# Half of the down projection's results added into SBUF by accumulating DMAs

## The chip, the cores and the metric

The kernel runs on one core of a Trainium2 chip. The time is device time in microseconds (us) of one execution. Before the change the median of 3 runs is 921.73 us (920.55 to 922.61).

## The reference

Attention with capped scores, then a mixing of tokens, then a feed-forward block with a residual, in float32 on 4 batches, 12 heads, 448 tokens and head width 64 (model width 768, hidden width 3072):

```
scores = cap * tanh(scale * q @ k.T / cap)          # per batch and head, 448 x 448
attn   = exp(scores - max) / (sum + 1e-9)
x      = (attn @ v) as [batch, 448, 768]
u      = x + (x.T @ U @ V).T                        # U: 448 x 32, V: 32 x 448
out    = u + relu(u @ w_ch1) @ w_ch2                # w_ch1: 768 x 3072, w_ch2: 3072 x 768
```

## The kernel before

The result of each batch b is built in one SBUF tile `u_bufs[b]`, 128 partitions x 6 slices d x 448 tokens, float32; slice d holds 128 of the 768 features. Attention and mixing fill it, and the feed-forward block adds to it in place, chunk by chunk.

The hidden width is cut into 24 blocks f of 128, and these into 12 chunks c of two (`CF`). For each chunk the up products make g = relu(...), 128 x 448, kept as a high and a low part, and the down products multiply the two blocks of w_ch2 with them. A down product of one d is 6 matmuls into one PSUM bank (`products`, L823: two f, and for each high x high, high x low, low x high). Its result is then added by VectorE to slice d (`add`, L828). This is done in two passes. In the plain pass (n = 0, batches 0 and 1) `moe` makes, for each chunk and batch, the up products of both f (`up_plain`, L738, 18 matmuls each), and between them all six down products of the chunk and batch before. In the Strassen pass (n = 1, batches 2 and 3) `up_seven` makes the up products of both batches and both f by seven products (L759, 9 matmuls each) with combinations on VectorE (L771, L776), and after each of them two of the twelve down products of the chunk before are taken. After the last chunk of a pass (`last`) each slice is stored (L834).

PSUM has eight banks. In the plain pass three of them (`pm`) serve the up and down products; in the Strassen pass five more (`pl`) join them. g is made by ScalarE (relu, high part) and VectorE (low part, L723). In the plain pass each weight block is decoded from 64-bit words by VectorE and ScalarE (L270 to L283), split into high (L229 on ScalarE) and low (L654), and written to DRAM (`kept`), from where the Strassen pass reads it again (L617).

Attention of batches 0 and 1 comes first; that of batches 2 and 3 is woven into the plain pass, a pair of heads every 50 us in the plan. The normalisation of a pair is a chain on GpSimd's DMA queue: four transfers of the sums into r (L480), VectorE's reciprocal (L490), one transfer to DRAM, rd (L485), and four broadcast loads, rb (L498). VectorE multiplies u by rb (L502), and then TensorE transposes u for the mixing (L525).

The order of instructions on every engine is drawn up beforehand. Each piece of work is a task with the engines it can run on and an assumed duration in ns, the buffers that it reads and writes, and a priority (smaller first). `simulate` plays the tasks through, engine by engine, and a task starts only when its buffers are free; the kernel then issues everything in that order. Each engine works through its own queue in order, so an instruction that waits holds up those behind it. The add has priority -200, ahead of all else:

```
self.task({"DVE": 622}, add, r=[(ps, 0)], w=[(u, d)], prio=-200)
```

Of the kernel before, what the change touches and what calls it, by code (L numbers as in the profile page):

```python
# [11 lines left out]
F32 = mybir.dt.float32  # L12
# [4 lines left out]
ALU = mybir.AluOpType  # L17

B, H, S, D = 4, 12, 448, 64
# [20 lines left out]
class Pool:  # L40


    def __init__(self, name, bufs, after=(), space=None, side=None):
        self.name, self.bufs, self.after, self.space, self.side = name, bufs, after, space, side
        self.free = dict(bufs)
        self.due = 0
        self.stack = self.pool = None
# [188 lines left out]
class Build(Plan):  # L236
    def __init__(self, tc, qk, v, u, vv, w1, w2, cap, ident, out):
        super().__init__()
        self.tc, self.nc = tc, tc.nc
        self.qk, self.v, self.u, self.vv = qk, v, u, vv  # L240
        self.w, self.cap, self.id_dram, self.out = (w1, w2), cap, ident, out
        PSUM = bass.MemoryType.PSUM
        self.cp = Pool("cp", {"const": 1})
        self.up = Pool("up", {"u%d" % b: 1 for b in range(B)})
        self.wp = Pool("wp", {"wa": 2, "w1": 3, "g": 3})
        self.wq = Pool("wq", {"wr": 2, "w0": 2})
        self.pre = Pool("pre", {"th": 4, "qk": 1, "es": 2})
        self.hp = Pool("hp", {"hl": 2}, after=(self.pre,))
        self.ap = Pool("ap", {"qk": 3, "vn": 2, "th": 3, "es": 2, "sr": 1, "r7": 2, "rb": 2, "xh": 1, "xl": 1, "ys": 1},
            side="right")  # L250
        self.xp = Pool("xp", {"x": 4, "ws": 3, "g": 3, "wa": 1}, after=(self.hp, self.wq))
        self.late = Pool("late", {"x": 3, "ws": 4, "cx": 4, "ta": 3}, after=(self.ap,), side="right")
        self.px = Pool("px", {"sc": 1, "s": 1}, space=PSUM, side="right")
        self.ps = Pool("ps", {"sc": 1, "o": 1, "misc": 2}, space=PSUM)
        self.pm = Pool("pm", {"mm": 3}, after=(self.px,), space=PSUM, side="right")
        self.pl = Pool("pl", {"mm": 5}, after=(self.ps,), space=PSUM)
        self.dp = None
# [421 lines left out]
    def moe(self):  # L679
# [4 lines left out]
        for n, bs in enumerate(((0, 1), (2, 3))):  # L684
            xs = self.operands(bs) if n else {b: self.halves(b) for b in bs}
            for c in range(NCH):
                fs = [c * CF + i for i in range(CF)]
                begin, prio = (12000, ALONE - 4 - 100) if n == 0 and c == 0 else (0, 3)
                ws = self.strassen_weights(c, prio) if n else {f: self.weights(0, f, True, begin, prio) for f in fs}
                w1 = {f: self.weights(1, f, n == 0, begin, prio) for f in fs}  # L690
                gs = {}
                if n:
                    down = self.down(order, *pend) if pend else iter(())
                    if c == 0:
                        for _ in down:
                            pass
                        order += 12
                    for _ in self.up_seven(bs, fs, xs, ws, gs, order):
                        next(down, None)
                        next(down, None)  # L700
                    for _ in down:
                        pass
                    pend = bs, fs, w1, gs, c == NCH - 1, n
                    order += 20
                    continue
                for b in bs:
                    for i, f in enumerate(fs):
                        self.up_plain(b, f, xs[b], ws[f], gs, order, n)
                        order += 1
                        if i == 0 and pend:  # L710
                            for _ in self.down(order, *pend):
                                pass
                            order += 12
                    pend = (b,), fs, w1, gs, c == NCH - 1, n
# [95 lines left out]
    def down(self, order, bs, fs, w1, g, last, n):  # L810
        nc = self.nc
        for i, b in enumerate(bs):
            u = self.u_bufs[b]
            for d in range(ND):
                k = ND * i + d
                at = order + 1 + k // 2 * 3 + k % 2
                ps = self.bank(n)
                sl = slice(128 * d, 128 * d + 128)

                def products(ps=ps, sl=sl, b=b):  # L820
                    for f in fs:
                        for i, (wi, gi) in enumerate(((0, 0), (0, 1), (1, 0))):
                            nc.tensor.matmul(  # L823
                                ps.t[:, :S], w1[f].t[:, wi, sl], g[b, f].t[:, gi], start=f == fs[0] and i == 0,
                                stop=f == fs[-1] and i == 2)

                def add(ps=ps, d=d, u=u):
                    nc.vector.tensor_tensor(out=u.t[:, d], in0=u.t[:, d], in1=ps.t[:, :S], op=ALU.add)  # L828

                self.task({"PE": 6 * 206}, products, r=[(x, i) for f in fs for x in (w1[f], g[b, f]) for i in range(2)],  # L830
                    w=[(ps, 0)], prio=at, mode="mm")
                self.task({"DVE": 622}, add, r=[(ps, 0)], w=[(u, d)], prio=-200)
                if last:
                    self.task({"SP": 350}, lambda b=b, d=d, u=u: nc.sync.dma_start(  # L834
                        out=self.out[b, 128 * d:128 * d + 128], in_=u.t[:, d]), r=[(u, d)], lat=2500, prio=-200)
                yield
# [56 lines left out]
```

## Time and profile before

| | before |
|---|---|
| median of 3 runs | 921.73 us |
| span of the profiled execution | 921.8 us |
| TensorE (PE) matmuls busy | 898.0 us, 97% |
| VectorE (DVE) busy | 714.1 us, 77% |
| ScalarE (ACT) busy | 379.9 us, 41% |
| GpSimd (POOL) busy | 60.5 us, 7% |
| bytes moved by DMA | 104.58 MB |

The profile is of one execution; its own time is the span of 921.8 us, which is within the spread of the runs. Busy time is the time in which an engine had an instruction in work; matmuls overlap, so a row's mean duration of a matmul is longer than the time from one to the next. A row of the tables by stage has the stretch in us, the busy time of each engine with the number of its instructions in brackets, the granted TensorE clock as a share of full speed (PEclk), the mean share of time in which the 16 DMA engines were busy, and GB/s. A line of the timeline has the start, the duration, the engine, the line of the kernel, the operation, what it writes and reads, and in square brackets the idle time before it and what ended it.

### The profile page before, as it was taken

What the parts mean: (1) busy time and instruction counts of PE and PEld (TensorE: products, weight loads), DVE (VectorE), ACT (ScalarE), POOL (GpSimd) and SP (SyncE); (2) the same over time, 40 slices, a digit from 0 to 9 for tenths busy, and PEclk for the clock granted to TensorE, in tenths of its full rate; (3) what the DMA queues carried; (4) which work ended last, traced back from release to release, by engine and by line L of the source; (5) the groups of instructions that cost most, each with busy time, mean ns of one, the idle gap of its engine ahead of it and who ended that gap; (6) DMA issues with size and microseconds to landing.
All of it is one profiled execution on the core that took longest, in us unless ns stands there. A gap on an engine that the chain in (4) does not pass through costs nothing.

```text
span 921.8 us, 11491 instructions
## 1 busy us (share of the span) xinstructions
PE 898.0 (97%) x4428; PEld 704.5 (76%) x4428; DVE 714.1 (77%) x1119; ACT 379.9 (41%) x513; POOL 60.5 (7%) x112
## 2 busy tenths in 40 slices
PE   6999999999999998999999999899999999999998
PEld 2233375767767666599999998799999999999997
DVE  5798896887887876778898775977777777777755
ACT  6988755545354541724323232512332222332210
POOL 0322210101011111020000000000000000000000
PEclk9999999999999998999999999999999999999999
DMA  7546330545434426145445433221121121122103
GB/s 255 173 153 204 92 101 32 163 175 169 167 125 149 138 61 211 66 137 181 121 156 190 163 103 123 100 72 67 52 69 56 48 61 60 52 69 67 38 1 120
DMA packets 34262, 104.58 MB, mean 113 GB/s; under 512 B 6192, under 2 KB 10272, under 8 KB 34208
## 3 DMA queue, kind: packets, MB, share of 16 engines
q1 hardware_dynamic: 23072, 79.29, 27.6%
q10 hardware_dynamic: 6912, 18.88, 5.1%
q0 software_dynamic: 4224, 5.68, 2.2%
q8 instruction: 35, 0.57, 0.3%
q14 instruction: 19, 0.16, 0.1%
HBM read 79.28 MB, written 24.47 MB: 113 GB/s over the span
## 4 chain that ended last, share of the span: by engine, by line
PE 90%; DMA 4%; DVE 4%; issue 1%; ACT 1%; POOL 0%; SPq 0%; DVEq 0%; POOLq 0%
PE mm L823 37%; PE mm L738 18%; PE mm L759 15%; PE sc L396 7%; PE o L436 4%; PE misc L436 2%; PE o L423 2%; PE misc L540 2%; DMA qk<-in_qk 1%; PE misc L525 1%; DMA r<-sr 1%; DMA rb<-rd 1%; DMA rd<-r 1%; PE misc L561 1%; PE misc L475 1%
## 5 line engine op out<-in xcount | busy, mean ns | idle before, releaser
L823 PE MATMUL mm<-g,w 128*128 128x448 f32 x1728 | 376.3, 368 | 0.5 <-DVE g L723 0.4
L823 PEld LDWEIGHTS mm<-g,w 128*128 128x128 f32 x1728 | 322.3, 188 | 44.5 <-issue 8.2
L828 DVE TENSOR_TENSOR u<-u,mm 128x448 f32<-128x448 f32 x288 | 177.7, 622 | 54.5 <-PE mm L823 50.5
L738 PE MATMUL mm<-hl,w 128*128 128x448 f32 x864 | 189.4, 371 | 0.0
L738 PEld LDWEIGHTS mm<-hl,w 128*128 128x128 f32 x864 | 160.2, 189 | 28.9 <-issue 14.9
L759 PE MATMUL mm<-x,ws 128*128 128x448 f32 x756 | 166.4, 368 | 3.7 <-DVE ws L597 3.6
L759 PEld LDWEIGHTS mm<-x,ws 128*128 128x128 f32 x756 | 142.4, 189 | 16.9 <-DVE ws L597 4.4
L401 ACT ACTIVATE th<-sc 128x896 f32<-128x896 f32 x84 | 75.2, 917 | 57.5 <-PE sc L396 43.4
L396 PE MATMUL sc<-qk 64*128 64x448 f32 (+1 forms) x384 | 87.1, 595 | 7.3 <-DVE qk L376 6.1
L229 ACT ACTIVATE w<-wa 128x768 fp32r<-128x768 f32 x72 | 59.4, 838 | 57.3 <-PE mm L823 35.7
L409 ACT ACTIVATE th<-th,capt 128x1792 f32<-128x1792 f32 (+1 forms) x48 | 76.7, 1603 | 0.7
L771 DVE TENSOR_TENSOR cx<-cx,mm 128x448 f32<-128x448 f32 x60 | 37.2, 620 | 45.8 <-PE mm L759 45.8
L654 DVE TENSOR_TENSOR w<-wa,w 128x768 fp32r<-128x768 f32 x72 | 68.6, 952 | 1.3 <-ACT w L229 0.3
L270 ACT ACTIVATE wa<-wr 128x768 f32<-128x768 f32 (+2 forms) x50 | 44.8, 896 | 55.7 <-DVE w L654 43.1
L274 DVE TENSOR_SCALAR wr<-wr 128x768 uint16<-128x768 uint16 (+2 forms) x50 | 50.6, 1024 | 17.1 <-DMA wr<-in_w 14.9
L396 PEld LDWEIGHTS sc<-qk 64*128 64x128 f32 (+1 forms) x384 | 27.1, 178 | 41.9 <-issue 14.7
L445 DVE TENSOR_TENSOR es<-es,th 128x896 f32<-128x896 f32 (+1 forms) x48 | 52.1, 1084 | 6.8 <-ACT th L409 6.3
L229 ACT ACTIVATE ws<-ta 128x384 fp32r<-128x384 f32 x39 | 20.3, 523 | 75.6 <-PE mm L759 69.3
L279 DVE TENSOR_SCALAR wr<-wr 128x768 uint16<-128x768 uint16 (+2 forms) x50 | 50.7, 1022 | 0.2
L229 ACT ACTIVATE g<-mm 128x448 fp32r<-128x448 f32 x48 | 26.1, 543 | 60.1 <-PE mm L738 60.1
L436 PE MATMUL o<-th,vn 128*64 128x448 f32 x216 | 47.5, 561 | 3.3 <-ACT th L409 3.0
L283 DVE SCALAR_TENSOR_TENSOR wa<-wa,wr 128x768 int32<-128x768 int32 (+2 forms) x50 | 46.5, 931 | 2.6 <-ACT wa L270 2.4
(77 smaller groups left out, 597.3 us busy)
## 6 DMA issues: line engine op xcount, KB each, us to landing
wr<-in_w SPq DMA_DIRECT2D x48, 768.0 KB, 5.5
kept<-wa ACTq DMA_DIRECT2D x48, 384.0 KB, 5.7
wa<-kept SPq DMA_DIRECT2D x48, 384.0 KB, 3.1
qk<-in_qk SPq DMA_DIRECT2D x24, 448.0 KB, 5.8
vn<-in_v SPq DMA_DIRECT2D x12, 448.0 KB, 7.3
rb<-rd POOLq DMA_DIRECT2D x48, 112.0 KB, 3.8
out_t<-u SPq DMA_DIRECT2D x24, 224.0 KB, 1.9
r<-sr POOLq DMA_DIRECT2D x48, 1.8 KB, 2.7
```

What stands on the lines that cost most here:

```text
L229: e.activation(out=out, in_=in_, func=func)
L279: nc.vector.tensor_scalar(out=half[:, 1::4], in0=half[:, 3::4], scalar1=0x8000, scalar2=None, op0=ALU.bitwise_and)
L396: nc.tensor.matmul(ps.t[out, a, :S], qks[c].t[hd, 1, 128 * t:min(S, 128 * t + 128)], qks[c].t[hd, 0], start=True, stop=True)
L401: nc.scalar.activation(out=th.t[:, j], in_=ps.t[:, :, :S], func=AF.Tanh)
L409: nc.scalar.activation(out=th.t[:, :n], in_=th.t[:, :n], func=AF.Exp, scale=self.capt)
L436: nc.tensor.matmul(o.t[64 * a:64 * a + 64, :S], vn.t[:, 3 * i + t, a], th.t[:, j, a], start=t == 0 and not late, stop=t == 2 and late)
L445: e.tensor_tensor(out=out(), in0=in0(), in1=in1(), op=ALU.add)
L654: e.tensor_tensor(out=w.t[:, 1], in0=a.t, in1=w.t[:, 0].bitcast(F32), op=ALU.subtract)
L738: nc.tensor.matmul(ps.t[:, :S], w.t[:, wi, sl], hl.t[:, xi, d], start=d == 0 and i == 0, stop=d == ND - 1 and i == 2)
L759: nc.tensor.matmul(ps.t[:, :S], ws[p].t[:, wi, sl], xs[p].t[:, xi, d], start=n == 0, stop=n == 8)
L823: nc.tensor.matmul(ps.t[:, :S], w1[f].t[:, wi, sl], g[b, f].t[:, gi], start=f == fs[0] and i == 0, stop=f == fs[-1] and i == 2)
L828: nc.vector.tensor_tensor(out=u.t[:, d], in0=u.t[:, d], in1=ps.t[:, :S], op=ALU.add)
```

## The change

Where d is odd and the chunk isn't the last of its pass, the result of the down product is copied by ScalarE from PSUM to a staging tile `st` (two of them, 128 x 448 float32, in the pool `wp`), and a DMA issued by GpSimd adds the staging tile into slice d of u in SBUF. The plan counts 560 ns of ScalarE for the copy, 1100 ns of GpSimd for the issue, and 3000 ns until the sum has landed. All other results are added by VectorE as before.

```diff
-        self.wp = Pool("wp", {"wa": 2, "w1": 3, "g": 3})
+        self.wp = Pool("wp", {"wa": 2, "w1": 3, "g": 3, "st": 2})
...
-                self.task({"DVE": 622}, add, r=[(ps, 0)], w=[(u, d)], prio=-200)
+                if d % 2 and not last:
+                    st = self.buf("st", [128, S], F32, self.wp)
+
+                    def pour(st=st, d=d, u=u):
+                        nc.gpsimd.dma_start(out=u.t[:, d], in_=st.t, accum_op=ALU.add)
+
+                    self.task({"ACT": 560}, lambda st=st, ps=ps: self.copy(nc.scalar, st.t, ps.t[:, :S]), r=[(ps, 0)],
+                        w=[(st, 0)], prio=-200)
+                    self.task({"POOL": 1100}, pour, r=[(st, 0)], w=[(u, d)], lat=3000, prio=-200)
+                else:
+                    self.task({"DVE": 622}, add, r=[(ps, 0)], w=[(u, d)], prio=-200)
```

## Rows read from the trace of the kernel before

**Rows 1.** Page, part 1: busy us, share of the span, instructions.
```profile
PE 898.0 (97%) x4428; PEld 704.5 (76%) x4428; DVE 714.1 (77%) x1119; ACT 379.9 (41%) x513; POOL 60.5 (7%) x112
```
**Rows 2.** Table by stage: woven stage, plain pass alone, Strassen pass.
```profile
130.00:420.00 290.00, 285.57 (x1424) 203.55 (x1423) 222.78 (x310) 132.73 (x163) 30.47 (x54) 0.99 0.42 136
420.00:575.00 155.00, 154.91 (x761) 142.45 (x760) 125.35 (x184) 48.49 (x72) 0.00 (x0) 1.00 0.45 147
603.00:903.00 300.00, 300.00 (x1473) 276.39 (x1472) 225.01 (x404) 78.20 (x136) 0.00 (x0) 1.00 0.18 54
```
**Rows 3.** Table by stage: 5 us stretches around two gaps of TensorE.
```profile
355.00:360.00 5.00, 2.85 (x14) 2.16 (x12) 2.49 (x5) 0.00 (x0) 0.00 (x0) 1.00 0.58 136
360.00:365.00 5.00, 3.88 (x11) 2.05 (x12) 4.92 (x10) 2.25 (x3) 0.00 (x0) 0.58 0.01 3
365.00:370.00 5.00, 5.00 (x22) 3.63 (x21) 1.79 (x3) 1.79 (x2) 0.00 (x0) 0.73 0.74 236
595.00:600.00 5.00, 1.35 (x6) 0.94 (x5) 5.00 (x11) 3.60 (x7) 0.00 (x0) 0.98 0.26 79
600.00:605.00 5.00, 5.00 (x19) 4.52 (x18) 3.65 (x7) 0.95 (x2) 0.00 (x0) 0.68 0.53 167
```
**Rows 4.** Timeline from 335 to 362 us, the lines of one normalisation chain.
```profile
343.64 0.56 POOL L485 DMA_DIRECT2D rd<-r  x1 [4.43 <-DVE r L490]
...
350.28 2.54 POOL L498 DMA_DIRECT2D rb<-rd  x4 [6.08 <-DMA rd<-r]
...
357.51 0.62 DVE L502 TENSOR_TENSOR u<-u,rb 128x448 f32<-128x448 f32 x1 [4.42 <-DMA rb<-rd]
...
358.28 0.29 PE L525 MATMUL misc<-ident,u 128*112 128x128 f32 x1 [0.73 <-DVE u L502]
...
359.96 0.61 DVE L502 TENSOR_TENSOR u<-u,rb 128x448 f32<-128x448 f32 x1
```
**Rows 5.** Table by stage: the stretch in which rb was on its way.
```profile
350.00:355.00 5.00, 5.00 (x26) 4.47 (x26) 3.10 (x5) 0.85 (x1) 2.54 (x4) 1.00 1.01 397
```
**Rows 6.** Timeline from 572 to 606 us, TensorE at the second gap's end.
```profile
599.41 2.69 PE L759 MATMUL mm<-x,ws 128*128 128x448 f32 x7 [3.65 <-DVE ws L597]
```
**Rows 7.** Page, part 5: group, count, busy us, mean ns, idle before it.
```profile
L828 DVE TENSOR_TENSOR u<-u,mm 128x448 f32<-128x448 f32 x288 | 177.7, 622 | 54.5 <-PE mm L823 50.5
```
**Rows 8.** Groups by line, ScalarE, 580 to 900 us.
```profile
L229 ACT ACTIVATE cx<-mm 128x448 f32<-128x448 f32 x24 | 13.1, 545 | 41.4 <-PE mm L759 41.4
```
**Rows 9.** Chain that ended last, one piece (start, us), and timeline, one exp.
```profile
431.17 7.30 PE mm L823 x36
...
213.01 1.79 ACT L409 ACTIVATE th<-th,capt 128x1792 f32<-128x1792 f32 x1
```
**Rows 10.** Groups by line, GpSimd, the whole span.
```profile
L480 POOL DMA_DIRECT2D r<-sr x48 | 26.7, 563 | 246.9 <-ACT sr L229 176.7 <-DVE sr L231 70.1
```
**Rows 11.** Instructions of tile rb: from issue to landing of its loads.
```profile
DMA to landing us min/median/max: 2.6/3.8/7.4
```
**Rows 12.** Page, part 6: DMA issues, count, KB each, median us to landing.
```profile
wa<-kept SPq DMA_DIRECT2D x48, 384.0 KB, 3.1
...
out_t<-u SPq DMA_DIRECT2D x24, 224.0 KB, 1.9
r<-sr POOLq DMA_DIRECT2D x48, 1.8 KB, 2.7
```
**Rows 13.** Timeline from 94 to 98.5 us, GpSimd and VectorE.
```profile
94.45 3.48 POOL L480 DMA_DIRECT2D r<-sr  x4 [6.06 <-ACT sr L229]
94.96 1.90 DVE L274 TENSOR_SCALAR wr<-wr 128x768 uint16<-128x768 uint16 x2
```
**Rows 14.** Timeline from 905 to 910 us, stores and adds of the last chunk.
```profile
905.97 3.34 SPq L834 DMA_DIRECT2D out_t<-u  x4
907.11 0.62 DVE L828 TENSOR_TENSOR u<-u,mm 128x448 f32<-128x448 f32 x1 [0.60 <-PE mm L823]
```

## The prediction

> **What bounds the kernel now.** The page's busy times come first: TensorE is busy for 898.0 us of the span of 921.8, VectorE for 714.1 [rows 1]. The change lightens the second, so the question is where TensorE waits at all, and for whom. The table by stage answers the first half. From 420 to 575 us (the plain MoE pass) TensorE is busy for 154.91 of 155.00 us with 761 matmuls, from 603 to 903 us (the Strassen pass) for 300.00 of 300.00 with 1473, which is 203.6 and 203.7 ns each, although VectorE is 81% busy in the first stage and 75% in the second, and the DMA share is 0.45 and 0.18 [rows 2]. In these 455 us no work taken from VectorE can be turned into time: TensorE doesn't wait for it, and its rate doesn't move with the DMA traffic.
>
> What is left are short gaps. Between 130 and 420 us, where attention of the last two batches is woven into the MoE, TensorE is idle for 4.4 us in all [rows 2], of which 2.15 + 1.12 = 3.27 us lie between 355 and 365 us. Behind that gap the granted clock has a mean of 0.58 and then 0.73 over 5 us each, so it is at the lower of its two levels (1.2 GHz) for a good part of them; that loses 2.10 + 1.35 = 3.45 us more, 6.7 us together. At the change to the Strassen pass it is the same: 3.65 us idle from 595 to 600 us and 0.32 x 5 = 1.6 us of low clock behind it, 5.25 us [rows 3]. The timeline says who was late. Before the first gap GpSimd issues rd at 343.64 and can issue rb only at 350.28, when rd has landed; rb releases the multiply L502 at 357.51, and the transposes L525 start behind it [rows 4]. The DMA share is 1.01 from 350 to 355 us [rows 5]: a chain of small GpSimd transfers runs beside big loads. The second gap waits on VectorE's subtraction L597 for the weights of the second Strassen chunk [rows 6].
>
> **The change part by part.** Of 288 adds (L828, 0.622 us) the 24 of the two last chunks stay, and half of the other 264 go: 132 x 0.622 = 82.1 us off VectorE [rows 7]. TensorE isn't waiting for VectorE where they lie, so I count 0. The gap at 595 us stays: VectorE is full there (5.00 of 5.00 us [rows 3]) with operands, subtractions and combinations; the adds shortly before it belong to a last chunk, and the first add of the Strassen pass comes after it.
>
> ScalarE gets 132 reads from PSUM, 66 in each pass (11 chunks x 6). Its read of the same shape into SBUF takes 0.545 us [rows 8], so 132 x 0.545 = 71.9 us, 36 in each. It was busy for 132.7 + 48.5 = 181 us of 445 in the plain pass and 78.2 of 300 in the other [rows 2]; 49% and 38% will do: hidden, 0 us. What it could cost is a PSUM bank. The plain pass has three, a down product (6 matmuls) takes 7.30 / 6 = 1.22 us, and a bank is needed again two products later, after 2.43 us. The read takes 0.545 of that, so it may start up to 1.89 us late; the longest thing that can stand ahead of it on ScalarE, an exp of four blocks, takes 1.79 us [rows 9]. It just fits: 0, with a few tenths now and then as the upper end.
>
> GpSimd gets 132 DMA issues. Its issues take 0.563 us on average [rows 10], 74 us in all; in the Strassen pass it does nothing now. The slowest group seen, 3.48 us for four [rows 13], would make 115 us of it, still hidden.
>
> The accumulate itself isn't in this trace: how long is it from issue to landing? The same 224 KB stored plainly by SyncE take 1.9 us, which is the lower end; the longest landing of a GpSimd load, 7.4 us, is the upper one [rows 11, 12]. Between them: GpSimd's SBUF to SBUF transfer takes 2.7 us with hardly any bytes in it, and 384 KB take 3.1 - 1.9 = 1.2 us more than 224, so 224 KB are worth 1.7 us. That makes an estimate of 4.4 us, or 6.1 if the destination, which is read as well, counts once more. I take 4.4. There are two staging tiles, and d = 1, 3, 5 follow each other by 2.43 us, so the read of d = 5 starts unhindered if the transfer of d = 1 has landed 4.87 - 0.545 - 0.1 (my allowance for two handovers) = 4.2 us after its issue. At 4.4 us ScalarE waits for 0.2, at 7.4 us for 3.2. Behind it in ScalarE's queue stands the relu of the next up product, which is due 18 matmuls or 3.65 us after d = 5. The next down product starts 7.30 us after d = 5 and uses that g three matmuls later, at 7.9. Between them go the read, the relu and VectorE's part of g, each of the size of the reads and adds above: 7.9 - 3 x 0.58 - 0.2 leaves 6.0 us of room. Only a landing beyond some 10 us reaches TensorE. In the Strassen pass such reads are 4.5 us apart, and the room is wider. So 0.
>
> By the Trainium skill's DMA page (DMA: Bandwidth & Descriptors, Anatomy of one DMA) a GpSimd transfer takes about 2.0 us plus its bytes over 436 GB/s; for 224 KB that is an estimate of 2.5 us, and ScalarE would never wait. The rows say 2.7 for next to no bytes and up to 7.4 beside loads [rows 11, 12], so by this trace it is too low.
>
> The SBUF page of the Trainium skill (SBUF — State Buffer, Who interferes with whom) speaks against the change: to issue a DMA, GpSimd writes descriptors to SBUF, and VectorE in a two-port mode locks it out for the whole instruction. One group of four issues took 3.48 us beside two tensor_scalars of VectorE, against 4 x 0.563 = 2.25 [rows 10, 13]. The trace would allow it; at some 0.3 us an issue it stays inside the 6.0 us of room and adds nothing to the sum.
>
> Does an add wait for a transfer into another d of the same tile? In the last stage the store of a slice, issued at 905.97, lands 1.9 us later, and the next slice's add starts at 907.11, having waited for TensorE alone [rows 12, 14]. Slices are kept apart: 0.
>
> What isn't settled by size is order. GpSimd's queue and its ring now carry transfers of 224 KB among the normalisation's chains of r, rd and rb, of which six start after 130 us, and the planner draws a new order of all engines. One chain of the six stalls TensorE now, for 6.7 us. A transfer ahead of a link costs it 0.56 us of issue and up to 1.7 us of data. The other way, VectorE comes to its multiplies sooner: the two L502 of the stalled chain lie 2.45 us apart [rows 4], for two instructions of 0.6 us in themselves. Bounds: -6.7 (no chain stalls) to +13.4 us (two more do). I take one stall as now, 0.
>
> Sum: 921.8 + 0 = 922 us; the span of the profiled execution, 921.8, is also the median of the runs (921.73).
>
> **The rivals.** *Faster, the stall goes.* A new order moves the chain away from the loads at 350 us, and a lighter VectorE closes it sooner: 921.8 - 6.7 = 915.1 us. For it: five chains of six didn't stall, and a gap that closes gives back the low clock behind it too. Against: nothing in the change shortens the chain's transfers, and it puts more on their queue. 0.29.
>
> *Slower, the chains stall more often.* An accumulate stands ahead of a chain's link in GpSimd's order, and waits there for its read on ScalarE, which waits for TensorE; then its data run ahead of the link's on the ring. One more stall gives 928.5, two more 935.2 us. It decides from about 3 us added to a chain: in the stalled one rb took 7.2 us where its median is 3.8 [rows 4, 11]. Two accumulates ahead, 2 x (0.56 + 1.7) = 4.5 us, are enough. Against: the planner counts 1.1 us of GpSimd for each, twice what an issue takes, and puts the chain's users accordingly later. 0.27.
>
> *Slower, the accumulate is slow.* Where it lands later than 10 us, each of the 22 rounds of the plain pass loses what is over: at 12 us 22 x 1.8 = 40 us, so 962 us. Against it stands the longest landing of 7.4 us [rows 11]; for it, that no transfer here reads its destination. 0.06.
>
> **How the numbers follow.** The forecast has 0.38, faster 0.29, the two slower ones 0.33. The runs of this kernel spread over 2 us, so 0.2%, 1.8 us, is about what a measurement can tell from no change, and the forecast's own range is 920 to 924. The range of 8 in 10 reaches down to the faster case and a little below, 914, and up to two more stalls, 936; the slow accumulate is left outside.
>
> **What would show it.** Each step: TensorE at about 203.6 ns per matmul from 420 to 575 us and in the Strassen pass, without idle time; 156 adds left on VectorE; 132 reads of 0.545 us on ScalarE; the accumulates landing after 4 to 7 us. The verdict lies in the gaps between 130 and 420 us and the granted clock behind them: none of 3 us is the faster case, two or more the slower. ScalarE waiting for a staging tile for over 6 us, or TensorE waiting for g or a bank in the plain pass, would show that I mis-sized the landing; another rate per matmul would show that the accumulate takes something from TensorE that plain transfers don't.

## The result, and the profile after

The changed kernel takes 930.69 us (median of 4 runs, 930.07 to 932.56) against 922.17 us (4 runs), a ratio of 1.0094 [1.0075, 1.0112]: slower by 8.5 us. The span of its profiled execution is 928.5 us, 6.7 us more than before. (That execution's own time is 930.35; the spans of these four runs stand 1.8 to 2.5 us below their times, so spans are compared with spans here. I had taken the span of before for its time.)

Busy times of the changed kernel, page, part 1:
```profile
PE 897.0 (97%) x4428; PEld 701.2 (76%) x4428; DVE 640.0 (69%) x986; ACT 447.9 (48%) x646; POOL 183.4 (20%) x244
```
Against [rows 1] VectorE lost 74 us and ScalarE and GpSimd took 68 and 123 us over; TensorE's work is the same. The table by stage of the changed kernel, for the stretches of [rows 2]:
```profile
130.00:420.00 290.00, 283.69 (x1423) 202.19 (x1422) 202.34 (x273) 151.97 (x199) 69.46 (x92) 1.00 0.59 166
420.00:575.00 155.00, 148.84 (x725) 134.28 (x724) 105.80 (x148) 59.81 (x96) 26.26 (x28) 1.00 0.67 178
603.00:903.00 300.00, 296.88 (x1450) 273.40 (x1451) 189.43 (x344) 114.46 (x206) 55.84 (x64) 0.99 0.47 104
```
The woven stage makes as many matmuls as before (1423 against 1424). From 420 to 575 us there are 725 instead of 761: 36 x 0.2036 = 7.3 us. (Up to 130 us the changed kernel had made 7 matmuls more, 601 against 594.) The Strassen pass only seems to lose, because the gap at its start has moved in. TensorE goes on behind it at 606.12 us instead of 599.41 [rows 6], 6.7 us later, and that is the difference of the spans. So it was all lost before. The line of the changed kernel (timeline, TensorE):
```profile
606.12 2.98 PE L759 MATMUL mm<-x,ws 128*128 128x448 f32 x7 [3.64 <-DVE ws L597]
```

Three stretches of the changed kernel, the same table:
```profile
360.00:365.00 5.00, 3.78 (x18) 2.31 (x16) 3.90 (x8) 2.59 (x4) 0.00 (x0) 1.00 0.70 186
365.00:370.00 5.00, 5.00 (x27) 3.24 (x28) 2.64 (x4) 3.78 (x5) 0.91 (x1) 1.00 0.65 208
605.00:610.00 5.00, 3.88 (x12) 3.51 (x13) 4.76 (x9) 1.89 (x4) 0.00 (x0) 0.66 0.21 51
```
The stall at 355 us with its 6.7 us is gone [rows 3]; what is left there is 1.22 us without a low clock. The gap at the change of passes is as before. In place of the one long stall there are many short ones. TensorE's gaps in the plain stretch of the changed kernel (timeline, TensorE, those with idle time before them):
```profile
426.88 0.65 PE L561 MATMUL misc<-vst,ys 128*128 128x448 f32 x2 [0.59 <-DVE ys L552]
...
465.56 1.50 PE L823 MATMUL mm<-g,w 128*128 128x448 f32 x6 [0.21 <-DVE u L828]
...
481.23 1.48 PE L823 MATMUL mm<-g,w 128*128 128x448 f32 x6 [0.53 <-DVE u L828]
...
493.70 5.22 PE L823 MATMUL mm<-g,w 128*128 128x448 f32 x24 [1.26 <-DVE g L723]
...
507.59 5.63 PE L823 MATMUL mm<-g,w 128*128 128x448 f32 x26 [0.40 <-DVE g L723]
...
514.21 1.48 PE L823 MATMUL mm<-g,w 128*128 128x448 f32 x6 [0.99 <-DVE u L828]
...
526.61 5.13 PE L823 MATMUL mm<-g,w 128*128 128x448 f32 x24 [1.18 <-DVE g L723]
...
546.40 1.48 PE L823 MATMUL mm<-g,w 128*128 128x448 f32 x6 [0.97 <-DVE u L828]
```
They add up to 6.1 us, and VectorE is named in each: after the first, which is of the mixing, either g or the add that frees a bank comes late. VectorE is not busier, it waits. Waits from 420 to 575 us, in the changed kernel (sum in us, times, longest):
```profile
DVE wr L274 <- DMA wr<-in_w: 27.3, 13, 3.4
...
ACT st L229 <- DMA u<-st: 19.1, 4, 5.7
ACT wa L270 <- DMA kept<-wa: 15.6, 5, 4.2
```
and in the kernel before:
```profile
DVE wr L274 <- DMA wr<-in_w: 8.0, 9, 2.8
...
ACT wa L270 <- DMA kept<-wa: 4.5, 1, 4.5
```
Not all of this is the transfers' doing. The same plan and the same reads with no transfer behind them (e3, below) have most of the waits for the weights as well:
```profile
DVE wr L274 <- DMA wr<-in_w: 19.7, 12, 3.3
...
ACT wa L270 <- DMA kept<-wa: 11.5, 4, 4.0
```
Six of the seven gaps behind that of the mixing, 5.1 us of the 6.1, follow a wait of VectorE for a weight load, 1.5 to 3.4 us long; ahead of the two longest ScalarE also waits for a write of kept, 4.2 us each. One of the six (changed kernel, timeline from 510 to 515 us, VectorE):
```profile
512.69 1.02 DVE L274 TENSOR_SCALAR wr<-wr 128x768 uint16<-128x768 uint16 x1 [2.65 <-DMA wr<-in_w]
513.51 0.65 DVE L828 TENSOR_TENSOR u<-u,mm 128x448 f32<-128x448 f32 x1
```
The add that frees the bank stands behind the decoding in VectorE's queue, and TensorE's 0.99 us before 514.21 end with it.

How a late landing of an accumulate gets from ScalarE to TensorE is seen in the woven stage (timeline of the changed kernel from 303 to 315 us, ScalarE, GpSimd, TensorE):
```profile
303.85 0.93 POOL L836 DMA_DIRECT2D u<-st  x1
...
311.99 0.54 ACT L229 ACTIVATE st<-mm 128x448 f32<-128x448 f32 x1 [4.27 <-DMA u<-st]
312.43 0.91 ACT L401 ACTIVATE th<-sc 128x896 f32<-128x896 f32 x1
...
313.39 1.02 PE L396 MATMUL sc<-qk 64*128 64x448 f32 x4 [1.84 <-ACT th L401]
```
The accumulate issued at 303.85 lands 8 us later; the read that needs its staging tile holds ScalarE's queue for 4.27 us, a tanh stands behind it, and the scores, which need that tanh's bank, start 1.84 us late. In the plain stretch it is weights that stand behind such a read (ScalarE, timeline from 492 to 512 us):
```profile
502.78 0.55 ACT L229 ACTIVATE st<-mm 128x448 f32<-128x448 f32 x1 [5.75 <-DMA u<-st]
503.22 0.84 ACT L229 ACTIVATE w<-wa 128x768 fp32r<-128x768 f32 x1
505.08 0.93 ACT L270 ACTIVATE wa<-wr 128x768 f32<-128x768 f32 x1 [1.03 <-DVE w L654]
505.91 0.53 ACT L229 ACTIVATE g<-mm 128x448 fp32r<-128x448 f32 x1
...
507.44 0.54 ACT L229 ACTIVATE g<-mm 128x448 fp32r<-128x448 f32 x1 [1.00 <-DVE wa L283]
```
The high part of a weight block (503.22) starts when the read is through, the decoding of the next block follows, and only behind those come the two relus. For VectorE's part of the first one's g TensorE waits 0.40 us at 507.59. Of the seven gaps this is the one that directly follows a staging tile.

### The profile page after: what moved, and what is told of

It reads as the page before. It is cut to its first block, busy times and chain, and to the rows that moved or that the text cites. A ratio compares the mean times of both kernels' runs of the same rounds, so it can differ in the third digit from the quotient of the medians.

```text
span 928.5 us, 11813 instructions
## 1 busy us (share of the span) xinstructions
PE 897.0 (97%) x4428; PEld 701.2 (76%) x4428; DVE 640.0 (69%) x986; ACT 447.9 (48%) x646; POOL 183.4 (20%) x244
## 4 chain that ended last, share of the span: by engine, by line
PE 69%; issue 13%; DMA 8%; DVE 5%; POOL 3%; ACT 1%; POOLq 0%; SPq 0%; DVEq 0%; ACTq 0%
PE mm L823 28%; PE mm L759 15%; PE mm L738 9%; PE sc L396 7%; PE o L436 4%; DMA u<-st 2%; POOL u L836 2%; DMA wr<-in_w 2%; PE o L423 1%; PE misc L540 1%; DMA qk<-in_qk 1%; PE misc L436 1%; DMA r<-sr 1%; PE misc L525 1%; DMA rb<-rd 1%
## 5 line engine op out<-in xcount | busy, mean ns | idle before, releaser
L836 POOL DMA_DIRECT2D u<-st x132 | 120.6, 913 | 566.6 <-ACT st L229 549.9
L229 ACT ACTIVATE st<-mm 128x448 f32<-128x448 f32 x132 | 71.9, 545 | 190.7 <-PE mm L823 146.5
L828 DVE TENSOR_TENSOR u<-u,mm 128x448 f32<-128x448 f32 x156 | 96.9, 622 | 26.3 <-PE mm L823 24.4
L274 DVE TENSOR_SCALAR wr<-wr 128x768 uint16<-128x768 uint16 (+2 forms) x50 | 50.8, 1023 | 50.7 <-DMA wr<-in_w 48.7
```

The lines of the kernel that those rows point to most:

```text
L229: e.activation(out=out, in_=in_, func=func)
L836: nc.gpsimd.dma_start(out=u.t[:, d], in_=st.t, accum_op=ALU.add)
```

## The experiments

Theories at the outset: A, the new order costs the time; B, late landings hold ScalarE up at the two staging tiles; C, the traffic of the accumulates delays the weight loads; D, the issues on GpSimd delay the normalisation. All ratios are to the kernel before on the same chip, whose median in the three groups was 922.3, 922.6 and 921.4 us, and 922.2 beside the last run.

**Old order, with reads and accumulates (e1).** The add's place in the plan of before, filled with the two new instructions:
```diff
 def add(ps=ps, d=d, u=u):
-    nc.vector.tensor_tensor(out=u.t[:, d], in0=u.t[:, d], in1=ps.t[:, :S], op=ALU.add)
+    if d % 2 == 0 or last:
+        nc.vector.tensor_tensor(...); return
+    st = self.opened(self.wp).tile([128, S], F32, tag="st", name="st", bufs=2)
+    self.copy(nc.scalar, st, ps.t[:, :S])
+    nc.gpsimd.dma_start(out=u.t[:, d], in_=st, accum_op=ALU.add)
```


> The 132 reads on ScalarE and the 132 accumulates are made, but in the order of the kernel before: each stands where the add stood in the plan, and TensorE's order is that of before. Theory A (the new order costs the time: weight decoding is planned closer to the landing of its loads, and what stands behind it on VectorE and ScalarE comes late): 918 to 925 us, with about 155 us of 155 busy in the plain stretch. Theory B (late landings hold up ScalarE at the two staging tiles, in whatever order): 928 to 935 us, ScalarE waiting for u<-st for 20 us or more in the plain pass. Theory C (the accumulates slow the loads of the weights): 926 to 932 us with landings of wr 1 us or more above before.

Measured 925.90 us, 1.0039 [1.0023, 1.0056]: less than half of the loss is there in the old order as well, with 24.9 us of waits for u<-st ahead of 582 us. Between the theories. By stage:
```profile
130.00:420.00 290.00, 283.49 (x1407) 200.04 (x1406) 201.19 (x269) 151.42 (x198) 63.52 (x90) 0.99 0.59 165
420.00:575.00 155.00, 154.33 (x759) 141.90 (x758) 109.92 (x153) 61.81 (x99) 28.47 (x30) 1.00 0.70 188
```
The accumulates cost the woven stage 2 us here, and the plain stretch next to nothing (0.67 us idle): in the old order it bears them.

**New order, adds on VectorE (e2).**
```diff
-self.task({"ACT": 560}, lambda st=st, ps=ps: self.copy(nc.scalar, st.t, ps.t[:, :S]), ...
+self.task({"ACT": 560}, lambda f=add: f(), ...
-                        nc.gpsimd.dma_start(out=u.t[:, d], in_=st.t, accum_op=ALU.add)
+                        pass
```


> The plan is that of the changed kernel, but VectorE makes all adds, each where the plan has the read on ScalarE; no staging, no accumulates. Theory A: 926 to 936 us, since the order is the new one and VectorE now also has 82 us of work that this plan doesn't count. Theories B and C: 919 to 925 us, since no landing and no added traffic is left.

Measured 922.15 us, 1.0002 [0.9986, 1.0017]. Theory A alone falls: the order by itself is no slower. By stage it isn't the same, though:
```profile
130.00:420.00 290.00, 287.16 (x1443) 205.18 (x1442) 223.53 (x315) 133.58 (x162) 31.41 (x54) 1.00 0.43 139
420.00:575.00 155.00, 152.14 (x743) 138.37 (x742) 121.61 (x179) 48.25 (x73) 0.00 (x0) 1.00 0.43 140
```
The stall at 355 us is gone, and 2.86 us of gaps in the plain stretch have come instead, without any accumulate. A part of them may belong to the adds that VectorE makes here and that this plan doesn't count; without those 1.6 us are left (e3). The new order is weaker just where the changed kernel loses.

**New order, reads on ScalarE, no transfers (e3).**
```diff
-                        nc.gpsimd.dma_start(out=u.t[:, d], in_=st.t, accum_op=ALU.add)
+                        pass
```


> The plan and the reads on ScalarE of the changed kernel, without the accumulates: the odd slices miss all sums but those of the two last chunks. Theory A: 927 to 932 us, as the changed kernel. Theory B: ScalarE can't wait for a landing any more, so 920 to 925 us. Theory C: the added traffic is gone, 920 to 925 us as well; B and C are told apart by the waits of the run in the old order.

Measured 917.57 us, 0.9953 [0.9938, 0.9968]: below all that was expected, and 4.6 us below the same order with adds. Without what the transfers bring, the change would have been a gain; they cost 930.69 - 917.57 = 13.1 us. By stage:
```profile
130.00:420.00 290.00, 288.23 (x1459) 208.46 (x1457) 207.83 (x280) 155.95 (x204) 31.14 (x54) 1.00 0.43 140
420.00:575.00 155.00, 153.39 (x751) 140.47 (x751) 110.26 (x158) 62.12 (x103) 0.00 (x0) 1.00 0.45 147
```

**The change in the Strassen pass alone (e4).**
```diff
-                if d % 2 and not last:
+                if d % 2 and not last and n:
```


> The change is made only in the Strassen pass; the plain pass is planned and run as before. All theories put the loss ahead of 582 us, into the woven stage and the plain pass, so 920 to 924 us, the same as before; anything over 926 us means that the Strassen pass loses too.

Measured 922.76 us, 1.0004 [0.999, 1.0019]. As expected: 66 of the 132 accumulates cost nothing and gain nothing, in a stage in which TensorE never waits.

**Three staging tiles (e5).** The plan still counts two; the tile ys shares the place of xl to make room:
```diff
-b.t = opened(b.pool).tile(b.shape, b.dtype, tag=b.tag, name=b.tag, bufs=b.pool.bufs[b.tag])
+if b.tag in ("xl", "ys"):
+    b.t = opened(b.pool).tile([128, 2, 256], b.dtype, tag="xl", name=b.tag, bufs=1)
+    b.t = b.t[:TM] if b.tag == "xl" else b.t[:, 0]
+else:
+    b.t = opened(b.pool).tile(..., bufs={"st": 3}.get(b.tag, b.pool.bufs[b.tag]))
```


> The changed kernel with its own plan, but with three staging tiles in SBUF instead of two (the plan still counts two), so that the read of d = 5 no longer waits for the accumulate of d = 1; traffic and order stay. Room for it comes from one small tile of the mixing step that shares the place of another. Theory B (ScalarE held up by the landing): the 36.5 us of ScalarE's waits for u<-st ahead of 582 us go, and the time comes to 919 to 924 us. Theory C (traffic of the accumulates delays the weight loads and the normalisation): waits for wr and gaps stay, 928 to 932 us. A share for each: between.

Measured 922.54 us (918.89 to 928.11), 1.0003 [0.9983, 1.0023]. Theory B takes 8.2 us of the 13.1: no wait for u<-st is left in the trace. The woven stage gets back 4 us, the plain stretch 1.6:
```profile
130.00:420.00 290.00, 287.65 (x1451) 206.96 (x1450) 205.21 (x276) 154.98 (x202) 71.19 (x93) 1.00 0.61 171
420.00:575.00 155.00, 150.45 (x731) 136.42 (x730) 107.26 (x152) 61.16 (x101) 25.71 (x27) 1.00 0.67 181
```
**Eight columns per accumulate (e6).**
```diff
-nc.gpsimd.dma_start(out=u.t[:, d], in_=st.t, accum_op=ALU.add)
+nc.gpsimd.dma_start(out=u.t[:, d, :8], in_=st.t[:, :8], accum_op=ALU.add)
```


> The changed kernel, but each accumulate carries only 8 of 448 columns (the rest of these sums is left out): the issues on GpSimd, their waits and the two staging tiles stay, the bytes go. Theory B and C: the landing falls to some 2.7 to 3 us and the traffic goes, so 916 to 920 us, as without any transfer. Theory D (the issues themselves cost: they stand ahead of the normalisation's transfers on GpSimd): 925 us or more.

Measured 921.28 us, 0.9983 [0.997, 0.9997]: between what B and C expected of it and what D did. The trace tells why. From issue to landing over the whole kernel (tile st):
```profile
DMA to landing us min/median/max: 2.0/2.0/8.9
```
Transfers of 4 KB land as late as 8.9 us, and ScalarE waits for them for 27.3 us ahead of 582 us, against 36.5 with all bytes. Such a landing isn't late because of its own size. It goes with the loads: the three latest were issued with four or five loads of 384 KB and more on their way, while in the Strassen pass, where the DMA share is 0.22, the latest takes 3.2 us. This wait, with the issues (median 0.869 us, as with all bytes), costs 2.8 us over the run without transfers by the ratios, 3.7 by the times, which come from two chips. D has no room beyond that.

**Overwrite instead of add (e7).**
```diff
-nc.gpsimd.dma_start(out=u.t[:, d], in_=st.t, accum_op=ALU.add)
+nc.gpsimd.dma_start(out=u.t[:, d], in_=st.t)
```


> The changed kernel, but the 224 KB transfer overwrites the slice instead of adding to it (these sums are left out): same bytes from the staging tile, no reading of the destination. If the adding is what makes the transfers long, the landing falls below 3 us, waits for u<-st to under 15 us, and the time to 918 to 923 us. If 224 KB on a loaded ring are long in any case, 926 to 932 us with landings as now.

Measured 922.51 us, 0.9999 [0.9988, 1.0011]. The time is the one expected if the adding is dear, the waits are not: 27.3 us, as with 4 KB. So adding costs 8.2 us more than writing the same bytes, and writing them costs 1.2 us more than 4 KB, hardly more than the measurement can tell. GpSimd's queue over the whole kernel (packets, MB, share of 16 engines) and the issues (count, KB, us to landing), first of the overwriting kernel, then of the changed one:
```profile
q0 software_dynamic: 12672, 35.97, 10.9%
...
u<-st POOLq DMA_DIRECT2D x132, 224.0 KB, 2.2
```
```profile
q0 software_dynamic: 23232, 35.97, 21.6%
...
u<-st POOLq DMA_DIRECT2D x132, 224.0 KB, 3.2
```
An accumulate needs 2.25 times the packets, twice the DMA engines' time, and 1 us more to land for the same bytes. (4224 packets of the queue belong to the normalisation.)

**GpSimd adds in SBUF (e8).**
```diff
-nc.gpsimd.dma_start(out=u.t[:, d], in_=st.t, accum_op=ALU.add)
+nc.gpsimd.tensor_tensor(out=u.t[:, d], in0=u.t[:, d], in1=st.t, op=ALU.add)
```


> The plan of the changed kernel, but GpSimd adds the staging tile to the slice itself, with an add in SBUF in place of the accumulating DMA: no traffic, no landing. If traffic and landing are the whole loss, 916 to 920 us, faster than both kernels. If GpSimd's add takes over 2.4 us, or VectorE's two-input work slows beside it, 924 us or more.

Measured 925.77 us, 1.0039 [1.0026, 1.0053]. The second branch: GpSimd's add isn't too long, but VectorE slows beside it. GpSimd's group over the whole kernel:
```profile
L836 POOL TENSOR_TENSOR u<-u,st 128x448 f32<-128x448 f32 x132 | 171.9, 1302 | 507.5 <-ACT st L229 507.4
```
and one of VectorE's from 130 to 575 us:
```profile
L274 DVE TENSOR_SCALAR wr<-wr 128x768 uint16<-128x768 uint16 x42 | 50.5, 1202 | 34.0 <-DMA wr<-in_w 33.8
```
The same 42 instructions take 1045 ns each in the changed kernel; VectorE's busy time from 130 to 575 us is 333.3 us here and 308.1 there. The Trainium skill's SBUF page (SBUF — State Buffer, Who interferes with whom) has VectorE and GpSimd share a pair of SBUF ports; these 25 us fit that. That they are the whole of the 8.2 us over the run with neither add nor transfer (e3) isn't shown.

**Old order, reads on ScalarE, no transfers (e9).** e1 without its last line.

> Order of the kernel before, the 132 reads made by ScalarE, no transfer behind them (these sums are left out). It shows whether the 4.7 us that the new order gained without transfers come from the order or from the adds that leave VectorE. If from VectorE's relief alone: 916 to 919 us here as well. If from the order (the stall at 355 us is gone there): the stall stays here and the time is 920 to 923 us.

Measured 919.97 us, 0.998 [0.9966, 0.9995], nearer to the second case: the stall at 355 us is there, though shorter (1.51 + 0.68 us idle). Taking the adds off VectorE is worth 0.2% or 1.8 us in the old order, by the ratio, and 4.6 in the new one (e3 against e2). And the transfers cost 5.4 us in the old order (e1 against this run, by the ratios), where they cost 13 in the new one.

**The kernel before, with later landings in its plan (e10).**
```diff
-self.task({"POOL": 1000}, put, ..., lat=2500, prio=prio)     # rd
+self.task({"POOL": 1000}, put, ..., lat=5000, prio=prio)
-self.task({"POOL": 2000}, get, ..., lat=2900, prio=prio)     # rb
+self.task({"POOL": 2000}, get, ..., lat=5500, prio=prio)
-self.task({"SP": 350}, load, w=[(raw, "u"), (raw, "l")], lat=4400, ...   # wr
+self.task({"SP": 350}, load, w=[(raw, "u"), (raw, "l")], lat=5600, ...
-self.task({"ACT": 120}, keep, ..., lat=5000, prio=prio)
+self.task({"ACT": 120}, keep, ..., lat=5800, prio=prio)
```


> The kernel before, all adds on VectorE, with the plan's landing times set nearer to what the traces show in this stage: rd 5.0 us after its issue instead of 2.5, rb 5.5 instead of 2.9, the weight loads 5.6 instead of 4.4, kept 5.8 instead of 5.0. If the stall at 355 us (6.7 us with the low clock behind it) comes from a plan that counts on early landings, it goes: 914 to 919 us, faster than both kernels. If the new plan only moves the stalls about: 920 to 926 us.

Measured 914.26 us (5 runs), 0.9917 [0.99, 0.9933]: faster than both kernels, and the fastest of all. Only the plan changed:
```profile
130.00:420.00 290.00, 287.29 (x1443) 207.19 (x1442) 226.68 (x315) 136.76 (x169) 27.50 (x50) 0.99 0.41 134
420.00:575.00 155.00, 154.72 (x769) 142.83 (x768) 128.07 (x192) 50.46 (x77) 2.51 (x4) 1.00 0.45 148
```
TensorE no longer waits for a normalisation chain, and VectorE waits for weight loads for 4.5 us from 130 to 582 us instead of 14.9.

**The changed kernel, with the same landings and 6.0 us for an accumulate (e11).** The four edits of e10, and:
```diff
-self.task({"POOL": 1100}, pour, r=[(st, 0)], w=[(u, d)], lat=3000, prio=-200)
+self.task({"POOL": 900}, pour, r=[(st, 0)], w=[(u, d)], lat=6000, prio=-200)
```


> The changed kernel with the same landing times in its plan, and 6.0 us instead of 3.0 for an accumulate. If a late landing costs because the plan doesn't count on it, ScalarE's reads are planned later, waits for u<-st fall from 36.5 us to under 15 us ahead of 582 us, and the time comes to 918 to 924 us. If two staging tiles are too few however they are planned, or the bytes themselves cost: 926 us or more.

Measured 917.95 us, 0.9951 [0.9933, 0.997]: 12.7 us less than the changed kernel, with every transfer still made. The profiled execution took 914.32 us, the shortest of the nine, so its rows don't show where the median loses.
```profile
130.00:420.00 290.00, 286.52 (x1441) 205.88 (x1441) 201.36 (x268) 157.18 (x211) 71.23 (x93) 1.00 0.59 162
420.00:575.00 155.00, 154.75 (x768) 142.86 (x767) 116.06 (x169) 65.47 (x106) 26.18 (x27) 1.00 0.69 190
```
Waits from 130 to 582 us:
```profile
DVE wr L274 <- DMA wr<-in_w: 15.9, 8, 4.5
...
ACT st L229 <- DMA u<-st: 3.9, 1, 3.9
```
In the changed kernel these waits are 48.7 and 36.5 us. The DMA share is as high as there (0.59 and 0.69) and the plain stretch is full again: most of the cost goes when the plan counts on later landings. Not all: against e10, which has the same landing times and no accumulates, this run is 3.1 us slower by the ratios, so the change doesn't pay in the repaired plan either.

**The changed kernel, with 6.0 us for an accumulate alone (e12).** The last edit of e11 without the four others.

> The changed kernel with only the accumulate's own times set in the plan: 0.9 us of GpSimd and 6.0 us until it has landed, instead of 1.1 and 3.0; all other times as they were. If the loss of the changed kernel came from its plan counting on early accumulates, the waits for u<-st fall under 15 us and the time is 918 to 924 us. If the repair in the run before came from the landing times of the weight loads and the normalisation, 926 to 932 us.

Measured 926.85 us (6 runs), 1.0054 [1.0037, 1.007], the second case: the accumulate's own times bring 3.8 of the 12.7 us, and the loads' and the normalisation's times the rest. Waits from 130 to 582 us:
```profile
DVE wr L274 <- DMA wr<-in_w: 46.1, 30, 3.3
ACT st L229 <- DMA u<-st: 13.4, 5, 4.1
```
The waits for u<-st fall as wished, those for the weight loads stay as they were.

## Why the prediction failed in its forecast

The time lies inside the range, but the forecast was no change, and it came out slower, for which the rivals together had 0.33. That it lies inside is luck: the upper part of the range was made of further stalls of the normalisation (928.5 for one more), and they are not what acted. The signs that I had named for a mis-sized landing came: TensorE waits for g and for banks in the plain stretch.

- *The step that failed* is "Only a landing beyond some 10 us reaches TensorE. ... So 0." The landings stayed below those 10 us, 3.1 to 8.9 us with 4.4 taken (median 3.2, and 3.8 from 130 to 575 us), though the longest went past my upper end of 7.4. The 6.0 us of room were wrong. I put one thing behind the waiting read on ScalarE, the relu. There are also the tanh of the woven attention, on whose bank the next scores wait at once, and the weights' high part and decoding, with VectorE in turn behind them. Landings of 8 us reach TensorE in both stages, for 1.84 and 0.40 us in the two timelines above. Freed of that wait (e5), the changed kernel is at 922.5.
- *No term for what the accumulates do to the rest of the traffic.* I allowed a transfer 1.7 us of ring time and asked only whom it delays among the normalisation. With and without bytes, with and without the wait, the new order takes 917.6 (neither), 921.3 (wait, 4 KB), 922.5 (bytes, no wait) and 930.7 us (both): by the ratios 2.8 and 4.6 us more than neither, each good to about 2 us, and 13.0 together. That each uses up slack that the other needs would explain the sum, but isn't shown. It isn't the bytes as such: written plainly, with the wait, they take 922.5 (e7). TensorE's idle time by stage in the profiled executions, in us, shows where each part acts:

| | woven stage | plain stretch |
|---|---|---|
| kernel before | 4.4 | 0.1 |
| new order, adds on VectorE (e2) | 2.8 | 2.9 |
| new order, no transfers (e3) | 1.8 | 1.6 |
| 4 KB each (e6) | 2.2 | 3.5 |
| plain writes (e7) | 1.9 | 4.7 |
| three staging tiles (e5) | 2.4 | 4.6 |
| changed kernel | 6.3 | 6.2 |

In the new order the woven stage loses only where accumulates meet two staging tiles. In the plain stretch the order has a part, and waits for weight loads carry most of it: of the 19 us by which VectorE's are longer than before, some 12 are there without any transfer (e3).

- *VectorE's relief at 0* was too little: 1.8 us in the old order (e9), 4.6 in the new one. That TensorE never waits for VectorE from 420 to 575 us was right of the old order only.
- *The order as a matter of chance*, from -6.7 to +13.4 us with 0 taken: the stall at 355 us did go, as the faster rival had it, and the new order still gained nothing (e2), because it gave the plain stretch 2.9 us of gaps. I had looked at the order in the woven stage alone. Both kinds of gaps go with the plan's landing times, which are too early: 2.5, 2.9, 4.4 and 5.0 us for rd, rb, wr and kept, where the kernel before has medians of 4.4, 4.4, 5.5 and 5.7 from 130 to 575 us (e10, e11). Each new setting also draws a new order, and only one order was run per setting, so a luckier order isn't ruled out; that the waits for the weights and the staging tiles shrink with it speaks for the landing times.
- *The slower chains* had a small part: the only gap of the changed kernel of this kind from 130 to 420 us is 1.73 us before 178.64, where one accumulate stands ahead of rb's issues and one among them. *The slow accumulate*, over 10 us, didn't occur.
- *Right*: the Strassen pass is untouched (e4; the 6.7 us are there at its start and at its end), the gap at the change of passes stays, slices are kept apart, the read takes 0.545 us, 156 adds stay. An issue takes 0.913 us on average, not 0.563, still hidden.

What stays open: how the cost of the accumulates without the wait (4.6 us) divides between later weight loads and later small transfers, and why wait and traffic together cost so much more than each alone. From 130 to 575 us the median landing of wr is 5.5 us before and 5.6 after, and only the longest grew much, from 7.6 to 8.7 us.

## What to carry to other kernels

Before an in-order engine gets an instruction that waits for a transfer, list everything in its queue behind it by stage, and give the room by the first of these that the bound engine needs, not by the one nearest in the same loop. Where an order is planned ahead, set the planned landing times from the trace of the loaded stage: here that alone was worth 7 us (e10, one new order), more than any work that was moved. And when a planned kernel changes, test the new order with the old work in it, and the old order with the new work: neither alone gave the result here.

## What the runs showed of the hardware

- An accumulating DMA of 224 KB in SBUF lands after 3.2 us (median of 132), a plain one after 2.2 (e7), one of 4 KB after 2.0 (e6); from 130 to 575 us, beside the loads, the medians are 3.8, 2.8 and 2.6, and the longest 8.9, 8.0 and 8.9. The accumulating one takes 144 packets instead of 64, and GpSimd 0.87 us to issue instead of 0.55 (medians). The 2.5 us that I had worked out from the Trainium skill's DMA page (DMA: Bandwidth & Descriptors, Anatomy of one DMA) are an estimate that lies between the plain and the accumulating median of the whole kernel; beside the loads the medians of both lie above it.
- GpSimd's own add of 128x448 float32 in SBUF takes 1.30 us, and one group of VectorE's 16-bit tensor_scalars (L274) went from 1.05 to 1.20 us in that run (e8).
- Gaps of 1.84 us and less left the granted clock at 1.00 in the woven stage and the plain stretch of the changed kernel (2.4 GHz); behind the gap of 3.64 us at the change of passes its mean was 0.66 over 5 us. Gaps hardly longer lost it in other runs: behind one of 1.99 us in the woven stage of e12 it was 0.78 and then 0.88 over 5 us each, and behind two of 1.51 and 0.68 us in close succession in e9 it was 0.69 over 5 us.
